# A gated-attention and low-rank-mixer kernel: another opening of the first batch, later loads of two weights, and an unspread closing of the last batch

## The chip, the cores and the metric

The kernel runs on one core of one Trainium2 chip. The time is device microseconds of one execution; the runs below are repeated executions of one program. Five engines work side by side, each with its own queue of instructions in program order: PE (matrix products, which write to PSUM), ACT and DVE (elementwise work, which read PSUM and SBUF), POOL (here it only issues transfers and fills small tiles) and SP (here it issues transfers, above all transposing ones). An instruction that waits for a semaphore holds up everything behind it on its own engine.

## The reference

Eight batches of 3136 rows; `u` and `v` are 256 wide, `z` 64 wide. All are float32 in memory.

```python
# per batch: attention without a softmax, gated by u
scores = (1 / S) * matmul(z, z.T)              # 3136 x 3136, symmetric
attn   = maximum(scores, 0.0) ** 2
x      = u * matmul(attn, v)                   # 3136 x 256
# then a low-rank mixer over the rows, and a two-layer channel network
h   = (x.T @ U @ V).T                          # rank 32
y   = x + h
out = y + maximum(y @ w_ch1, 0.0) @ w_ch2      # 256 -> 1024 -> 256
```

## The kernel before, in words

**Tiles.** The 3136 rows are 25 tiles: 24 full ones of 128 rows and a tail of 64. Row `p * 24 + t` of the first 3072 is row `p` of tile `t`. Everything is computed in bfloat16 with float32 sums.

**Panels and strips.** `attn` is symmetric, so the kernel makes only half of it. The panel of tile `j`, `A[j]`, holds the blocks of row tile `j` against column tiles `j` to `j + 12`, around the circle of 25. A step of `score` (L288 to L313) makes one piece of a panel: two matmuls into a pair of PSUM banks (L298), each using one half of PE's 128 rows, since `z` is 64 wide and stands twice in `zT`; then ACT's relu with the scale (L311) from PSUM to SBUF; then DVE's square in place (L313). There are two such PSUM pairs in turn (`pair_psum`), so the third `score` waits until ACT has read the first. The other half of an output's blocks comes from a strip: `turn` (L333) lets a transposing transfer on SP's queue turn the panel's twelve blocks beside the diagonal into a strip tile.

**Outputs.** Output tile `o` is the sum over 25 tiles `j` of a block (from a panel or from the strip of `o`) times `v[j]`, in matmuls of 64 rows by 256 columns (L371), one half of the rows into each of two PSUM banks. Two neighbouring outputs share a set of two banks; `close_pair` adds the banks (ACT's copy L385, DVE's add L386), multiplies by `u` (L395) and leaves `x_bf`. There are two such sets, `sets[0]` and `sets[1]`. Outputs go in the order 12, 13, ..., 24, 0, ..., 11 (`turns`). Output 24 is the tail and runs as quarters (L405).

**Opening of batch 0** (`start_up`, L665). Seven matmuls on zeros; two thirds of `z` arrive as float32 by two transfers on SP's queue (`first_z`, L212), are cast and doubled by DVE (L215) and ACT (L216), and turned by PE against a unit matrix (`turn_on_pe`, L223); the last third comes through POOL's queue (`load_z`, L174). Outputs 12 to 15 are then summed over all 25 `j` from blocks that are made for them alone: for each pair in `pairs` one `score` of 512 columns for each `j`, against the columns of tiles 12 to 15. Blocks that belong to a panel go to their place in it; the others go to `rooms`, borrowed space in panels that are made later, and are made again when their panel is. The weights (`fetches`, L254 to L261) and the first parts of batch 1's `v` are loaded in this stretch, through POOL's queue. A one-row transfer on SP's queue (`mark`) waits for the third of these parts, and the strips stand behind it. Outputs 16 to 19 follow from stored panels and strips; batch 1's `z` is doubled (L188) and turned (L195) meanwhile.

**The rest.** From output 20 on, `attend_steps` runs output by output, with steps that make later panels spread among the sums (`first_at`, `own_at`, `next_at`), and with the mixer of the batch before in bursts: `up_steps` (L563, relu L571, L579 and L581) and `down_steps` (L610, the add L624, the store L637). A strip is turned four outputs ahead.

**Closing.** The last batch's own mixer has no attention beside it. `rank` (L462) makes `x.T @ U`, `mix` (L515, L522) corrects the turned `x` of chunk 0, and `low_rank` (L531, L545) adds the low-rank part to the `x` of a chunk in PSUM and SBUF and turns it for the up steps. Which PSUM banks `low_rank` uses, and where it stands among the up and down steps, is written out by hand:

```python
for c in range(NC + 1):
    up, down = last[c]
    steps = _merge(up, down)
    adds = {0: ((2, 2),), 1: ((0, 1), (3, 6))}.get(c, ((c + 2, 2),) if c + 2 < NC else ())
    for n, at in reversed(adds):
        steps.insert(at, lambda n=n: low_rank(b, n, other, n > 0))
    run(steps)
```

So chunk 0's add stands after chunk 1's first up step, in the banks of `other`. Two of chunk 0's four up steps (`alone`) use the banks of `spare()` instead of a `pair_psum`. The last chunk's down steps (`apart`) keep their two tiles in separate banks, with an add and a store for each.

Of the kernel before, what the change touches and what calls it, by code (L numbers as in the profile page):

```python
# [7 lines left out]
FP32 = mybir.dt.float32  # L8
# [34 lines left out]
def kernel(  # L43
# [17 lines left out]
    P = 128  # L61
# [138 lines left out]
    def first_z(parts):  # L200

        z_bf = z_tiles[0] = stage.tile([P, NT, 2, dqk], BF16, name="z_bf")
        wide = zT_rest[:, :4, :].rearrange("p t c -> p (t c)")
        nc.vector.memset(wide, 0.0)
        ps = pair_psum()
        for _ in range(7):
            mm(out=ps[:, 0, :], lhsT=zT_rest[:, 0, :], rhs=wide, start=True, stop=True)  # L207
        landed = []
        for t0, t1 in parts:
            z_f = u_pool.tile([P, 2, D], FP32, name="u_sb").rearrange("p a c -> p (a c)")  # L210
            z_f = z_f.rearrange("p (t c) -> p t c", c=dqk)
            nc.sync.dma_start(out=z_f, in_=rows(z[0])[:, t0:t1, :])  # L212
            landed.append(z_f)
        for (t0, t1), z_f in zip(parts, landed):
            nc.vector.tensor_copy(out=z_bf[:, t0:t1, 0, :], in_=z_f)  # L215
            nc.scalar.copy(out=z_bf[:, t0:t1, 1, :], in_=z_f)  # L216

    def turn_on_pe(parts, banks):

        z_bf = z_tiles[0]  # L220
        for (t0, t1), ps in zip(parts, banks):
# [8 lines left out]
            copy = nc.vector.tensor_copy if t0 % 8 or t1 == NF else nc.scalar.copy  # L230
# [21 lines left out]
    def weight_steps():  # L252
        def wide(w_bf, w):
            pool_dma(out=w_bf, in_=w.rearrange("(t p) d -> p t d", p=P))  # L254
# [19 lines left out]
        def copies():  # L274
            for n in (R, 2 * R):
                nc.vector.tensor_copy(out=V_bf[n : 2 * n, :], in_=V_bf[:n, :])

        fetches = [
            lambda: wide(w1_bf, moe_w_ch1),
            narrow,  # L280
            fetch,
            lambda: wide(w2_bf[:, NH // 2 :, :], moe_w_ch2[H // 2 :, :]),
            lambda: wide(w2_bf[:, : NH // 2, :], moe_w_ch2[: H // 2, :]),
        ]
# [302 lines left out]
    def down_steps(b, c):  # L587
# [10 lines left out]
        apart = b == B - 1 and c == NC - 1  # L598

        def step(n, k):  # L600
# [3 lines left out]
            ps = spare()[n] if apart and k else hold[0]  # L604
# [12 lines left out]
            if apart or k == len(pair) - 1:  # L617
                k0 = k if apart else 0
                t, nk = pair[k0], k + 1 - k0
                if k0 == 0:  # L620
                    hold[1] = out_pool.tile([P, 2, D], FP32, name="o_sb")
                o_sb = hold[1][:, k0 : k + 1, :]
                p = P if t < NF else TAIL
                nc.vector.tensor_tensor(  # L624
                    out=o_sb[:p].rearrange("p t (a c) -> p t a c", c=P),
                    in0=split(ps[:p, k0 * D : (k + 1) * D]),
# [9 lines left out]
                if t < NF:  # L636
                    store(out=rows(out[b])[:, t : t + nk, :], in_=o_sb)  # L637
                else:
                    store(out=out[b, NF * P :, :], in_=o_sb[:TAIL, 0, :])
# [24 lines left out]

    def start_up():  # L665
        parts = ((8, 16), (0, 8), (16, NF))
        first_z(parts[:2])
# [10 lines left out]
        load_v(0, (8, 12))  # L678
        load_v(0, (12, 18))
        load_z(0, parts[2:])  # L680
        for part in [(3, 8), (0, 3), (18, NF), (NF, NT)]:
            load_v(0, part)
        turn_on_pe([(8, 12), (12, 16)], sets[0])
        turn_on_pe([(0, 4), (4, 8)], sets[1])
        nc.gpsimd.memset(U_bf[:, NF, :], 0.0)
        outs = [FIRST + i for i in range(NG)]
        c0 = FIRST * P
        for o in outs[::2]:
            open_pair(0, o)
            load_u(0, o)  # L690
        if B > 1:
            load_z(1, WHOLE)
        run(fetches)
        if B > 1:
            for part in V_PARTS[:3]:
                load_v(1, part)
        nxt = [s for j in range(LEAD, LEAD + NG) for s in turned(0, j)]
        rooms = [A[j % NT][:, : 2 * NG * P] for j in range(LEAD + NG, LEAD + 3 * NG)]
        rooms = [r.rearrange("p (a w) -> p a w", a=2) for r in rooms]
        pairs = [(8, 9), (10, 11), (12, 13), (14, 15), (6, 7), (3, 4), (5,), (1, 2)]  # L700
        pairs += [(0, 16), (17, 18), (19, 20), (21, 22), (23, 24)]
        where = {}
        mark = small.tile([P, D], BF16, name="mark", tag="t1_sb")[:1, :8]

        def make(pair):
            if all(LEAD - 1 - HALF <= j < FIRST for j in pair):
                todo = []
                for j in pair:
                    at = (FIRST - j) * P
                    where[j] = A[j][:, at : at + NG * P]  # L710
                    todo.append((j, c0, NG * P, where[j]))
                score(0, todo)
            else:
                room = rooms.pop(0)
                for i, j in enumerate(pair):
                    where[j] = room[:, i, :]
                score(0, [(j, c0, NG * P, room) for j in pair])

        def use(pair, some):
            for j in pair:  # L720
                for o in some:
                    at = (o - FIRST) * P
                    stop = [o % 2 == 1 and j == NF - h for h in range(2)]
                    beside(o, j, where[j][:, at : at + P], stop)

        for i, pair in enumerate(pairs):
            if i == 5 and B > 1:

                nc.sync.dma_start(out=mark, in_=v_both[1][:1, V_PARTS[2][1] - 1, :8])
            if i == 3:  # L730
                double_z(0, parts[2:])
            if i == 5:
                turn_on_pe([(16, NF)], [pair_psum().rearrange("p a w -> p (a w)")])
                turn_on_pe([(NF, NT)], [pair_psum()[:, 0, :]])
                extend_z(0)
            make(pair)
            if i > 5 and i % 2:
                nxt.pop(0)()
            if i > 1:
                use(pairs[i - 2], outs)  # L740

        for o in outs[1::2]:
            nxt.pop(0)()
            for pair in pairs[-2:]:
                use(pair, (o - 1, o))
            close_pair(0, o)

        outs = [LEAD + i for i in range(NG)]
        for o in outs[::2]:
            open_pair(0, o)  # L750
            load_u(0, o)
        pairs = [(j, j - 1) for j in range(LEAD - 1, LEAD - FIRST, -2)]

        def use_stored(js, some):
            for j in js:
                for o in some:
                    if 0 <= o - j <= HALF:
                        beside(o, j, block(0, o, j))

        def make_stored(pair):  # L760
            todo = []
            for j in pair:
                k0, k1 = LEAD - j, min(NB, LEAD + NG - j)
                todo.append((j, LEAD * P, (k1 - k0) * P, A[j][:, k0 * P : k1 * P]))
            score(0, todo)

        nxt += [lambda pair=pair: make_stored(pair) for pair in pairs[:2]]
        run(nxt[:2])
        own = [
            lambda j=j, some=some: use_stored([j], some)  # L770
            for some in (outs[:2], outs[2:])
            for j in outs
            if j <= some[-1]
        ]
        run(_merge(nxt[2:], own))
        rest = []
        for j in reversed(range(FIRST - NG, LEAD)):
            rest += score_steps(0, j, LEAD + NG - j, NB)
        more = [s for j in range(LEAD + NG, LEAD + 2 * NG - 1) for s in score_steps(0, j)]
        for i, pair in enumerate(pairs):  # L780
            if i + 2 < len(pairs):
                make_stored(pairs[i + 2])
            else:
                more.pop(0)()
            use_stored(pair, outs)
            if B > 1 and i in (1, 2):
                part = ((0, FIRST), (FIRST, NF))[i - 1]
                double_z(1, (part,))
                turn_z(1, (part,))
            if i == len(pairs) - 1:  # L790
                turn(0, LEAD + NG)
        tail = []
        for o in outs:
            js = [(o + 1 + i) % NT for i in range(HALF)]

            def close(o=o, j=js[-1]):
                beside(o, j, block(0, o, j), [o % 2 == 1] * 2)
                if o % 2:
                    close_pair(0, o)
                if o == outs[1]:  # L800
                    load_u(0, LEAD + NG)
                if o < outs[-2]:
                    turn(0, o + NG + 1)

            for i in range(3):
                some = js[4 * i : min(4 * i + 4, HALF - 1)]
                tail.append(lambda o=o, js=some: [beside(o, j, block(0, o, j)) for j in js])
            tail.append(close)
        for s in _merge(tail, more + rest):
            s()  # L810
# [134 lines left out]
```

## Time and profile before

| | |
|---|---|
| Runs (us) | 1000.08, 1001.38, 1001.78; median 1001.38 |
| The profiled execution's own time | 1000.08 |
| Its span on the core | 998.3 |
| PE, ACT, DVE, POOL busy | 983.4, 612.2, 551.1, 171.7 |
| PE busy from 0 to 5 / 5 to 10 us | 3.75 / 4.04 |
| PE busy from 30 to 35 / 35 to 40 us | 5.00 / 4.94 |
| PE busy from 60 to 80 / 80 to 100 us | 19.45 / 20.00 |
| First cast of `z` (L215, L216) | 3.54 |
| First score pair (L298) | 6.06 |
| Closing of outputs 12-13 / 14-15 on ACT (L385) | 24.16 / 25.40 |
| First strip issued on SP's queue (L333) | 29.84 |
| Last closing of outputs 16-19 on ACT | 44.38 |
| Closing of output 24 on ACT | 65.39 |
| First matmul of `w2` (L610) | 123.88 |
| Last batch's first `rank` matmul (L462) | 943.48 |
| Issue of the last store | 995.38 |

Times count from the start of the span. PE's busy time is modelled and covers the pipeline's latency, so a window in which PE is full can still hold small gaps; a window in which it is not full holds a wait. A row of the profile gives the engine, the line, the operation, the tiles as `out<-in`, the shape, and in brackets how long the engine stood idle before it and what ended that. The numbers of a window are its length, then busy time and instructions of PE, PEld (the loading of PE's weights), DVE, ACT and POOL, the granted clock, the mean busy share of the transfer engines and GB/s.

### The profile page before, as it was taken

Reading aid. Unit: us, or ns where it says so; the run is one execution under the profiler, and the core shown is the slowest. Engines: PE = TensorE matmul, PEld = TensorE weight load, DVE = VectorE, ACT = ScalarE, POOL = GpSimd, SP = SyncE. Lnnn points to the kernel's source line nnn. Section 1 sums busy time; section 2 is a strip of 40 time slices with the busy share of each in tenths; the row PEclk is TensorE's granted clock in tenths of the full one; section 3 lists DMA queues with packets and bytes.
Section 4 is the critical chain, followed back from the end, with each engine's and each line's share of the span. In section 5 each row is a group of like instructions: output and inputs, shape, how many; then the busy total and the mean of one; then the engine's idle time right before and its main releaser. Section 6 shows DMA issues by size and latency. Waiting matters only on the chain.

```text
span 998.3 us, 31020 instructions
## 1 busy us (share of the span) xinstructions
PE 983.4 (99%) x13688; PEld 776.5 (78%) x13688; DVE 551.1 (55%) x1003; ACT 612.2 (61%) x835; POOL 171.7 (17%) x317
## 2 busy tenths in 40 slices
PE   8899999999999999999999999999999999999998
PEld 6678777787778877788787887878877788787866
DVE  6878754467444665456644566445664457542352
ACT  8877764667645776466754667556674666643154
POOL 5111112111121211221112211112111120011000
PEclk9999999999999999999999999999999999999999
DMA  9999989899798999999999997989979998678533
GB/s 195 185 195 204 174 156 186 185 176 173 153 198 171 169 157 186 179 178 169 160 180 176 181 168 149 188 174 177 175 151 194 166 188 159 120 150 161 129 95 101
DMA packets 414790, 167.94 MB, mean 168 GB/s; under 512 B 389488, under 2 KB 399408, under 8 KB 414656
## 3 DMA queue, kind: packets, MB, share of 16 engines
q1 hardware_dynamic: 385424, 99.68, 62.3%
q0 software_dynamic: 29232, 66.28, 28.3%
q8 instruction: 107, 1.75, 0.7%
q14 instruction: 27, 0.22, 0.1%
HBM read 61.88 MB, written 25.69 MB: 88 GB/s over the span
## 4 chain that ended last, share of the span: by engine, by line
PE 91%; DVE 4%; ACT 3%; DMA 1%; issue 1%; POOL 0%; DVEq 0%; POOLq 0%
PE ps L371 47%; PE ps L563 17%; PE ps L610 17%; PE ps L298 6%; ACT A L311 2%; DVE A L313 2%; PE ps L405 1%; PE ps L531 1%; DVE x_bf L545 1%; DMA out_dram<-o_sb 1%; DMA strip<-A 1%; DVE both L386 1%; PE ps L479 1%; DVE x_bf L395 1%; PE ps L207 0%
## 5 line engine op out<-in xcount | busy, mean ns | idle before, releaser
L311 ACT ACTIVATE A<-ps 128x832 bf16<-128x832 f32 (+9 forms) x477 | 358.9, 769 | 155.4 <-PE ps L298 148.1
L371 PE MATMUL ps<-v,A 64*128 64x256 bf16 x4988 | 341.6, 269 | 1.8 <-DVE A L313 1.1
L313 DVE TENSOR_TENSOR A<-A 128x832 bf16<-128x832 bf16 (+9 forms) x477 | 244.7, 527 | 133.1 <-ACT A L311 130.0
L371 PE MATMUL ps<-v,strip 64*128 64x256 bf16 x4420 | 307.3, 269 | 3.4 <-DMA strip<-A 2.5
L371 PEld LDWEIGHTS <-A 64*128 64x128 bf16 x4988 | 246.3, 94 | 45.4 <-issue 10.0
L581 ACT ACTIVATE relu_bf<-ps 128x1024 bf16<-128x1024 f32 (+2 forms) x206 | 186.2, 911 | 140.0 <-PE ps L563 139.8
L371 PEld LDWEIGHTS <-strip 64*128 64x128 bf16 x4420 | 222.6, 94 | 37.2 <-DMA strip<-A 3.9
L624 DVE TENSOR_TENSOR o_sb<-ps,x_bf 128x512 f32<-128x512 f32 (+2 forms) x105 | 69.9, 665 | 243.7 <-PE ps L610 221.7
L610 PE MATMUL ps<-w_bf,relu_bf 128*128 128x256 bf16 (+1 forms) x1600 | 201.2, 273 | 0.0
L563 PE MATMUL ps<-ut,w_bf 128*128 128x512 bf16 (+2 forms) x896 | 198.6, 353 | 0.0
L610 PEld LDWEIGHTS <-relu_bf 128*128 128x128 bf16 (+1 forms) x1600 | 153.0, 98 | 45.6 <-issue 3.6
L563 PEld LDWEIGHTS <-w_bf 128*128 128x128 bf16 x896 | 84.9, 98 | 62.0 <-issue 6.9
L355 POOL DMA_DIRECT2D u_sb<-in_u_dram x96 | 53.7, 559 | 456.1 <-DVE x_bf L395 441.9
L298 PE MATMUL ps<-zT 64*128 64x416 bf16 (+8 forms) x812 | 131.6, 312 | 0.0
L385 ACT COPY both<-ps 128x512 f32<-128x512 f32 (+1 forms) x104 | 58.9, 566 | 72.9 <-PE ps L371 66.6
L637 POOL DMA_DIRECT2D out_dram<-o_sb x84 | 46.0, 548 | 276.2 <-DVE o_sb L624 272.9
L386 DVE TENSOR_TENSOR both<-ps,both 128x512 f32<-128x512 f32 (+1 forms) x104 | 69.3, 667 | 28.2 <-ACT both L385 27.5
L395 DVE TENSOR_TENSOR x_bf<-both,u_sb 128x512 bf16<-128x512 f32 (+1 forms) x104 | 69.8, 672 | 3.7
L545 DVE TENSOR_TENSOR x_bf<-ps,x_bf 128x512 bf16<-128x512 f32 (+1 forms) x112 | 65.5, 626 | 7.2 <-PE ps L531 7.1
L298 PEld LDWEIGHTS <-zT 64*128 64x128 bf16 x812 | 43.1, 94 | 4.0
L244 POOL DMA_DIRECT2D v<-in_v_dram x61 | 34.1, 561 | 0.8 <-DMA w_bf<-in_moe_w_ch_dram 0.7
L298 PE MATMUL ps<-relu_bf 64*128 64x416 bf16 (+9 forms) x121 | 22.2, 333 | 3.9 <-ACT A L311 3.3
(54 smaller groups left out, 208.0 us busy)
## 6 DMA issues: line engine op xcount, KB each, us to landing
u_sb<-in_u_dram POOLq DMA_DIRECT2D x96, 256.0 KB, 4.1
out_dram<-o_sb POOLq DMA_DIRECT2D x84, 256.0 KB, 3.3
v<-in_v_dram POOLq DMA_DIRECT2D x57, 192.0 KB, 4.8
strip<-A SPq DMA_TRANSPOSE x196, 5.5
out_dram<-o_sb SPq DMA_DIRECT2D x11, 256.0 KB, 2.0
z_c<-in_z_dram POOLq DMA_DIRECT2D x7, 384.0 KB, 5.9
u_sb<-in_u_dram POOLq DMA_DIRECT2D x16, 64.0 KB, 2.5
ut<-x_bf SPq DMA_TRANSPOSE x56, 3.7
```

What stands on the lines that cost most here:

```text
L298: mm(out=ps[:, k, :n], lhsT=zT[halves[k], j, :], rhs=zT_flat[halves[k], c : c + n], start=True, stop=True,)
L311: nc.scalar.activation(out=dst, in_=src, func=AF.Relu, scale=sc)
L313: nc.vector.tensor_tensor(out=dst, in0=dst, in1=dst, op=ALU.mult)
L371: mm(out=acc[t0][h][:, (o - t0) * D : (o - t0 + 1) * D], lhsT=w[halves[h]], rhs=v_both[b % 2][halves[h], j, :], start=start, stop=stop, **kw,)
L385: nc.scalar.copy(out=both[:, :w], in_=banks[1][:, :w])
L386: nc.vector.tensor_tensor(out=both[:, :w], in0=banks[0][:, :w], in1=both[:, :w], op=ALU.add)
L395: nc.vector.tensor_tensor(out=x_at(b, t0, n), in0=split(both[:, :w]), in1=u_sb[:, :n, :].rearrange("p t (a c) -> p t a c", c=P), op=ALU.mult,)
L545: nc.vector.tensor_tensor(out=q, in0=split(ps[h][:, : len(ks) * D]), in1=q, op=ALU.add)
L563: mm(out=ps[i][:, :w] if apart else ps[:, i, :w], lhsT=w1_bf[:, db, (hp + i) * P : (hp + i + 1) * P], rhs=uT[c][:, db, len(chunks[c]) * P ...
L581: nc.scalar.activation(out=relus[c][:, hp : hp + 2, :w], in_=ps[:, :, :w], func=AF.Relu)
L610: mm(out=ps[r, k * D : (k + 1) * D], lhsT=relus[c][:, ht, q : q + (TAIL if two else P)], rhs=w2_bf[:, ht, :], start=(ht < 1 + two), stop=( ...
L624: nc.vector.tensor_tensor(out=o_sb[:p].rearrange("p t (a c) -> p t a c", c=P), in0=split(ps[:p, k0 * D : (k + 1) * D]), in1=x_at(b, t, nk) ...
```

## The change

The opening is written anew. `first_z` sends all of `z` by SP's and ACT's queues in turn, the tail too, and its casts come back as steps. Outputs 12 to 15 no longer get blocks of their own: their panels 12 to 15 are made in full, then the needed ends of panels 11 to 0, and tiles beyond each panel come from the strips of outputs 12 to 15, turned on SP's queue as soon as each panel is squared. `rooms` and `mark` are gone. Outputs 16 to 19 follow in the same way. Batch 1's `z` is doubled and turned at outputs 21 to 23 (steps 9 to 11 of the main loop) instead of in the opening. `w1` is fetched at output 7 (step 20), into the space of batch 0's `zT`, and two DVE copies at output 10 (step 23) put its columns in another order; `w2` is fetched in batch 1, eight neighbouring rows to each partition, in the order that fits those columns. In the closing, chunk 0's `low_rank` stands behind the first of its own up steps, in the banks of `spare()`, `mix` comes before the late down steps, and the last two tiles share one bank, one add and one store.

In batch 0 the program order has, of score matmuls, 22 fewer of 512 columns and 2 fewer of 448, and 15 more of 64-row shapes between 128 and 416 columns; 92 of the L371 matmuls read a strip instead of a panel; four more strips are turned.

```diff
     def first_z(parts):
...
-            nc.sync.dma_start(out=z_f, in_=rows(z[0])[:, t0:t1, :])
...
+        queues = (nc.sync.dma_start, nc.scalar.dma_start)
+        for n, (t0, t1) in enumerate(parts):
+            if t0 == NF:
+                z_f = both_pool.tile([P, 512], FP32, name="both")[:, :dqk]
+                for r in halves:
+                    queues[n % 2](out=z_f[r], in_=z[0, NF * P :, :])
+                z_f = z_f.rearrange("p (t c) -> p t c", t=1)
+            else:
+                pool, name = ((u_pool, "u_sb"), (out_pool, "o_sb"))[n % 2]
...
+                queues[n % 2](out=z_f, in_=rows(z[0])[:, t0:t1, :])
+
+            def cast(t0=t0, t1=t1, z_f=z_f, shared=n < 2):
+                nc.vector.tensor_copy(out=z_bf[:, t0:t1, 0, :], in_=z_f)
+                copy = nc.scalar.copy if shared else nc.vector.tensor_copy
+                copy(out=z_bf[:, t0:t1, 1, :], in_=z_f)
...
+        w1_tmp = idle[:, : ND * H].rearrange("p (a h) -> p a h", a=ND)
+        def first_w():
+            pool_dma(out=w1_tmp, in_=moe_w_ch1.rearrange("(t p) d -> p t d", p=P))
+        def second_w():
+            pool_dma(out=w2_bf, in_=moe_w_ch2.rearrange("(p t) d -> p t d", t=NH))
+        def order_w():
+            for a in range(ND):
+                nc.vector.tensor_copy(
+                    out=w1_bf[:, a, :].rearrange("p (t q) -> p t q", q=P),
+                    in_=w1_tmp[:, a, :].rearrange("p (q t) -> p q t", t=NH),
+                )
...
-        apart = b == B - 1 and c == NC - 1
...
-            ps = spare()[n] if apart and k else hold[0]
+            ps = hold[0]
...
+    def use_strip(o, part):
+        js = [(o + 1 + i) % NT for i in range(HALF)]
+        for j in js[4 * part : 4 * part + 4]:
+            end = j == js[-1]
+            beside(o, j, block(0, o, j), [end and o % 2 == 1] * 2)
+        if part == 2 and o % 2:
+            close_pair(0, o)
...
     def start_up():
-        parts = ((8, 16), (0, 8), (16, NF))
-        first_z(parts[:2])
+        casts = first_z(((8, 16), (16, NF), (0, 8), (NF, NT)))
...
+        run(casts[:2])
+        turn_on_pe([(8, 12), (12, 16)], sets[0], (act, vec))
+        turn_on_pe([(16, 20), (20, NF)], sets[1], (act, vec))
+        casts[3]()
...
+        run(fetches[:2])
+        panel = {o: turned(0, o) for o in range(FIRST, LEAD + NG + 1)}
...
+        make((8, 9), FIRST)
+        turn_on_pe([(NF, NT)], [sets[1][0]], (vec,))
+        casts[2]()
+        make((10, 11), FIRST)
+        steps = [panel[12][0], use((8, 9)), turn_rest, panel[12][1], use((10, 11))]
+        steps += [lambda: extend_z(0), lambda: make((6, 7), FIRST), panel[13][0], use((12,))]
+        steps += [panel[13][1], use((6, 7)), panel[14][0], use((13,)), panel[14][1]]
+        steps += [panel[15][0], use((14,)), panel[15][1], lambda: make((4, 5), FIRST), use((15,))]
+        steps += [lambda: make((2, 3), FIRST), use((4, 5)), lambda: make((0, 1), FIRST)]
+        steps += [use((2, 3)), *strip_steps(12), panel[16][0], use((0, 1)), *strip_steps(13)[:2]]
+        steps += [panel[16][1], strip_steps(13)[2], *strip_steps(14), panel[17][0]]
...
+    later = {(0, 20): fetches[2], (0, 23): fetches[3], (1, 1): fetches[4]}
...
     rank(b, other[0], 0, NT - 3)
-    run(late[: ups // 2])
+    run(late[: NH // 2])
     rank(b, other[0], NT - 3)
-    run(late[ups // 2 : ups])
+    run(late[NH // 2 : NH // 2 + 1])
     mix(b, 0)
+    run(late[NH // 2 + 1 :])
     low_rank(b, 1, other)
-    run(late[ups:])
     for c in range(NC + 1):
         up, down = last[c]
...
+        if c + 2 < NC:
+            up.insert(3 if c == 0 else 1, lambda c=c: low_rank(b, c + 2, other))
+        if c == 0:
+            up.insert(1, lambda: low_rank(b, 0, None, False))
+        run(_merge(up, down))
```

## The prediction

> **What bounds the kernel now.** I read the page's shares first: PE 99% busy, DVE 55%, ACT 61%, so nearly everywhere only PE's queue counts. Then, since the change lies at both ends, the waits of PE in the first 70 us (line waited for: total us, times, longest) and after them:
>
> ```profile
> PE ps L298 <- ACT A L311: 3.3, 5, 1.0
> PE ps L371 <- DMA strip<-A: 2.5, 1, 2.5
> PE ps L371 <- DVE A L313: 2.0, 4, 0.9
> ...
> PE ps L531 <- DVE x_bf L545: 1.1, 7, 0.2
> ```
>
> Most of what PE loses to waits, it loses in the opening: 3.3 on ACT, 2.0 on DVE, 2.5 on one strip. The windows show where (first PE busy, then PEld, DVE, ACT):
>
> ```profile
> 10.00:15.00 5.00, 4.59 (x72) 3.72 (x70) 4.90 (x11) 3.43 (x8) 3.31 (x6) 1.00 1.11 250
> 15.00:20.00 5.00, 4.40 (x66) 3.43 (x63) 3.26 (x5) 5.00 (x6) 3.36 (x7) 1.00 1.12 207
> 20.00:25.00 5.00, 4.42 (x69) 3.55 (x67) 3.48 (x6) 4.51 (x7) 1.52 (x3) 1.00 1.30 199
> 25.00:30.00 5.00, 3.64 (x38) 1.91 (x36) 4.93 (x10) 5.00 (x9) 1.09 (x2) 1.00 0.77 158
> ...
> 40.00:50.00 10.00, 6.91 (x114) 5.58 (x111) 6.88 (x15) 7.38 (x13) 1.61 (x3) 1.00 1.19 200
> ```
>
> ACT is full at 15-20 and 25-30, where PE has gaps; at 40-50 PE misses 3.1 us while ACT has room. The chain of waits names that gap, the strip of output 20:
>
> ```profile
> 41.20 0.51 DVE A L313
> 41.72 0.03 issue
> 41.75 0.27 DVE both L386
> 42.02 6.45 DMA strip<-A
> 48.47 0.05 issue
> 48.52 0.50 PE ps L371 x6
> ```
>
> Last the closing, in the timeline: PE never stops from 949.5, and the end is one add and one store.
>
> ```profile
> 947.52 1.23 DVE L522 TENSOR_TENSOR ut<-ps,ut 128x1024 bf16<-128x1024 f32 x1
> 948.66 1.28 DVE L545 TENSOR_TENSOR x_bf<-ps,x_bf 128x512 bf16<-128x512 f32 x2
> ...
> 994.93 0.42 DVE L624 TENSOR_TENSOR o_sb<-ps,x_bf 128x256 f32<-128x256 f32 x1 [0.52 <-PE ps L610]
> ```
>
> **The change, part by part.** Durations used: a long run of L371 matmuls takes 0.87 us per 16, so 0.0545 each; ACT on a 1024-wide PSUM pair 0.90 from start to start (three in 2.70), on 512 columns 0.48 (6.54, 7.04, 7.51, 7.99), 832 between them by width, 0.75, with 0.86 to its end; PE's score to ACT's start 0.4 (6.06 to 6.54; 48.86 to 49.24); the square of 832 0.59, of 512 0.42.
>
> *Work.* In batch 0 the order of instructions has 22 fewer score matmuls of 512 columns and 2 fewer of 448, and 15 narrower ones in their place: 6,912 columns less, two row halves at once, 3,456 / 2.4 per ns = 1.4 us of PE. ACT drops nine 1024s, four 512s and an 896 (10.8) and gains nine narrower (4.9): 5.9 us less. The 92 matmuls that go from panels to strips cost the same. None of this is a gain yet: what counts is when each queue gets through.
>
> *z.* The second piece goes out on ACT's queue at 0.80 instead of 1.24 on SP's. ACT issues three transfers before its table load. By SP's rows (0.39, 0.42) that is 1.2 us:
>
> ```profile
> 0.80 1.28 ACT L216 ACT_TABLE_LOAD   x1 [0.80 <-PEq L929]
> 0.80 0.86 SPq L212 DMA_DIRECT2D u_sb<-in_z_dram  x2
> 3.54 1.25 ACT L216 CAST z_bf<-u_sb 128x512 bf16<-128x512 f32 x2 [1.46 <-DMA u_sb<-in_z_dram]
> ```
>
> The cover is the 1.46 us that ACT idles for z: 1.2 fits with 0.2 left, price 0. Both z pieces now share the engines, so the first lands up to 0.6 later (the distance of the two landings before, 3.5 and 4.1), and the cast with it. Bounds: -0.4 (the saved issue) to +1.3 (cover gone, PE and all else waits for ACT's half of the cast); I take +0.3, near the late side of the landing.
> [...]
>
> *First four outputs (12-15).* I walked the queues from the first score pair at 6.06. The second pair now follows two 64-column casts on DVE (0.24 and 0.21, row L272), behind the copy that ends at 6.86: 7.3 instead of 6.3. The turn of z tiles 0-7 holds one of two PSUM pairs until DVE's 1024-column copy (1.22) ends at 11.4; ACT idles 1.1 and begins panel 13's stretch at 11.9. In panels 13-15 each later half stands on PE behind matmuls that read the half just made: 0.4 + 0.86 + 0.59 and 6, 4 or 2 matmuls, 2.2 a panel against 1.5 of ACT alone. So panel 15 is squared at 19.4, the last narrow pair leaves ACT at 21.6, and strips begin at 21.9: 4 x 23 strip matmuls and 6 others (5.3) and four score pairs (0.7) end at 28.0. Before, these outputs' accumulators close at 25.4. That is 2.6 later, but with panels 12-17 stored, most of which were made afterwards before.
>
> *Outputs 16-19.* 196 matmuls (10.7), 20 score pairs (3.1), and 3.2 of waits: the second accumulator set is free only after ACT's copy and DVE's add (28.3 + 0.58 + 0.69), and the two closings (1.3 each on DVE) hold back squares that PE is next in line for. End 45.0 against 43.95.
>
> *Outputs 20-24.* Strip 20's panel is squared at 38.5 instead of 42.0, so the 2.5 wait goes, and the one at 57.5 (1.2, strip 23). Before, 43.95 to 65.4 is 21.4; after, 21.4 - 2.5 - 1.2 - 0.4 (narrower panels 0-2, no panel 23) = 17.3. End 62.3 against 65.4: **-3.1**. What is late next: batch 1's z is doubled and turned at outputs 21-23 instead of in the opening, so DVE's copy of zT (L238) may wait some 3 us for its transfer. Behind it stand the squares of panels 6-11, the add of output 24, and ACT's copies L391; PE meets that only at the third score after it. Price 0, up to 2.
>
> *Strips under load.* Four strips now start at 12-20 us, beside POOL's loads of v, u, z, U and V. Issue to landing (min/median/max), for the strips issued at 29-41, no loads beside them, and at 76-92, loads beside them:
>
> ```profile
> DMA to landing us min/median/max: 3.8/5.3/5.9
> DMA to landing us min/median/max: 5.6/7.7/9.8
> ```
>
> Strip 12 goes out at 12.0 and is wanted at 21.9; 13 at 15.1 for 23.7; 14 at 17.4 for 25.2; 15 at 19.5 for 26.6. At 7.7 each all land in time (14 just); at 9.8 strips 14 and 15 are 2 to 3 late. w1 and w2, 1 MB between 19.4 and 26.1, are gone from here, which helps. I take +0.6, between 0 and 7.
>
> *w1, w2 late.* w1 lands in 7.0 (its rows before: 6.9 to 7.3) and is reordered three outputs later (3.1 each, 9.3). The reorder is two strided DVE copies, 1.1 each by the 768-column L265 row (0.82), beside gaps of about 1 us per square at 95-100; if that cover is gone, 2.2. w2 is wanted at the first L610 (123.9) and issued near 105. POOL's queue behind both holds u and v loads with a pair's lead. 0.
>
> *Closing.* Output chunk 0's adds move in front of its second up step, which uses the same two banks. DVE then has in order: the mix add (ends 949.5), an output add (0.69), chunk 1's two adds and chunk 0's two (0.60 apart): the bank is free at 951.9, PE wants it at 950.6. The wait of 1.3, less 0.1 of slack, is +1.2. PE, then all ups and downs, stand behind it. The last two tiles leave as one 512-wide add and one 256 KB store: 0.69 for 0.42, and 1.9 to 2.1 to landing for 1.7: +0.5. Together **+1.7**, bounds 0.5 (DVE ahead of my count) to 2.6.
>
> **Sum.** 0.3 - 3.1 + 0.6 + 1.7 = -0.5 on the profiled execution, 998.3 of span and 1.8 around it, 1000.08: 999.6. That execution was the fastest of three; their median is 1001.38, 1.3 higher. For a median of runs I name 1000.7.
>
> **Rivals.** *Faster:* ACT is the true bound of the opening. Then most of its 5.9 counts, say 5.0, and with z +0.3 and the closing's 1.7 the time is 3.0 lower: 1000.7 - 2.5 = 998.2, from there down to 996.8 if the closing costs only its 0.5. For it: ACT full at 15-20 and 25-30. Against it: my walk finds ACT idling about 4 us before 21.6, on DVE and PSUM.
> *Slower:* strips 13-15 come late. Strips issued at 77.9, 81.9 and 83.8 under load landed about 4 us apart; were 13, 14 and 15 to follow strip 12 (19.7) in such steps, 15 would land at 31.7, 5.1 after it is wanted. It decides once the steps exceed (26.6 - 19.7) / 3 = 2.3. Time 1000.7 + 5.1 - 0.6 = 1005.2. For it: DMA share 1.1 to 1.3 at 10-25. Against it: the landings with no loads beside them are 1.3 to 2.1 apart, and POOL's backlog should be gone by about 21.
> *It does not do what it says* (opening unchanged in time, later outputs waiting for strips as before): then only the closing shows, 1002.7. The earlier issue of strip 20 speaks against it.
>
> **How the numbers follow.** Forecast (the opening's gain and the closing's loss cancel to within a microsecond or two) 0.38; faster 0.28; slower by late strips 0.24; closing alone 0.10. About 0.2%, 2 us, is what a measurement here can tell from no change. "Closing alone" lies 1.3 above the median, so I count 0.06 of it within and 0.04 beyond: faster 0.28, same 0.38 + 0.06 = 0.44, slower 0.24 + 0.04 = 0.28. The range reaches to both rivals, 996.8 to 1005.2; the forecast's own is 998.7 to 1002.7.
>
> **What would show it.** Right: the accumulators of 12-15 close near 28, no wait of PE on a strip, first matmul of output 20 near 45, output 24's end near 62; near 950 a wait of PE's up step on L565's adds of about 1.2. Wrong: PE waiting for a strip between 22 and 28 (the slower rival), accumulators closing at 26 or sooner (the faster one), the first cast after 4.0 (the table load), DVE stalled at the reorder near 97.

## The result: 2.4% slower

The changed kernel takes 1026.07 us (median of 6 runs, 1021.51 to 1028.71) against 1000.88 (999.5 to 1004.02): ratio 1.0241, 95% interval 1.021 to 1.0272. The forecast was 1000.7. The profiled run of the changed kernel is its fastest, 1021.51 (span 1019.5).

First the waits of PE, as they were shown for before (line <- what it waited for: total us, times, longest):

```profile
PE ps L391 <- DMA strip<-A: 5.8, 4, 3.7
PE ps L425 <- DVE x_bf L565: 5.6, 5, 4.4
PE ps L318 <- ACT A L331: 2.8, 5, 1.1
PE ps L391 <- DVE A L333: 2.8, 6, 0.8
...
PE ps L583 <- DVE x_bf L565: 1.0, 1, 1.0
```

Strips are waited for four times instead of once (at 42.4, 56.9, 108.5 and 113.9 us; none of them at 22 to 28), and a new wait of 4.4 stands before L425, the matmuls of output 24, here of batch 1. The windows show where PE goes empty (PE, PEld, DVE and ACT busy; then POOL, granted clock, DMA share, GB/s):

```profile
15.00:20.00 5.00, 3.31 (x32) 1.67 (x32) 4.04 (x8) 5.00 (x9) 0.45 (x1) 0.88 1.29 144
20.00:25.00 5.00, 5.00 (x75) 4.64 (x73) 0.96 (x4) 1.49 (x4) 0.00 (x0) 0.77 1.21 253
...
40.00:50.00 10.00, 8.84 (x145) 7.33 (x144) 7.58 (x15) 7.80 (x13) 1.63 (x3) 1.00 1.18 220
100.00:110.00 10.00, 7.16 (x120) 5.89 (x115) 5.92 (x9) 4.88 (x7) 1.62 (x3) 1.00 1.31 132
110.00:120.00 10.00, 6.26 (x89) 4.27 (x88) 2.03 (x4) 2.41 (x4) 0.00 (x0) 0.83 1.09 160
160.00:200.00 40.00, 35.35 (x407) 26.74 (x405) 14.50 (x28) 15.99 (x23) 7.10 (x13) 0.91 0.87 152
```

At 40-50 PE gained 1.9 on before's 6.91, as forecast. But at 100-120 it misses 6.6 and at 160-200 4.7, where before had full rows. At 100-110 the DMA engines were busy (1.31) and moved only 132 GB/s. The chain of waits puts one strip there, and DVE's timeline three waits on late transfers. After the last of them come the low-rank adds (L565, from 179.10), and then PE's wait of 4.4:

```profile
96.35 17.54 DMA strip<-A
113.89 0.05 issue
```

```profile
66.22 0.56 DVE L250 COPY zT<-zT 128x1536 bf16<-128x1536 bf16 x1 [3.00 <-DMA zT<-z_bf]
...
102.50 2.10 DVE L277 COPY w_bf<-relu_bf 128x1024 bf16<-128x1024 bf16 x2 [2.56 <-DMA relu_bf<-in_moe_w_ch_dram]
...
178.63 0.56 DVE L250 COPY zT<-zT 128x1536 bf16<-128x1536 bf16 x1 [5.56 <-DMA zT<-z_bf]
```

```profile
179.84 0.37 PE L425 MATMUL ps<-v,A 64*64 64x256 bf16 x1 [4.42 <-DVE x_bf L565]
```

Waiting is not all of the loss. PE's busy time is 989.7 us against 983.4, although it has a little less to do. The granted clock of the changed kernel stood at 0.50 for 3.4 us from 18.8, for 3.4 from 114.4 and for 6.8 from 179.3, and at 1.00 otherwise from 6 us to the end of its last matmuls; before had 1.00 from 6 to 990. At 0.50 a 64x256 matmul of L391 took a mean of 412 ns (20.0 to 22.2), at 1.00 it took 269 from a strip (22.3 to 24.5). Half of these 13.6 us, 6.8, is an estimate of what the slower clock added to the 21.2 by which the span grew.

To place the loss, take for each pair of outputs the time at which DVE writes it to `x_bf` (L415; L395 before), changed minus before. Pair 0 is outputs 12 and 13 of batch 0, pair 6 is output 24, pair 13 begins batch 1, pair 103 is the last.

| pair | 0 | 1 | 3 | 5 | 6 | 11 | 13 | 17 | 18 | 20 | 103 | span |
|---|---|---|---|---|---|---|---|---|---|---|---|---|
| changed - before | +2.1 | +2.9 | +1.7 | -0.8 | +2.7 | +1.6 | +10.5 | +10.5 | +14.7 | +18.2 | +19.0 | +21.2 |

Four steps: +3.5 at output 24 (batch 1's z; 1.3 of it is gone again at pair 7), +8.9 at pairs 12 and 13 (w1, issued at 89.2), +7.7 at pairs 18 to 20 (batch 2's z, which the change also moves: loaded at output 17 of batch 1 instead of 13, and doubled and turned later), and +2.2 in the closing. At w1 PE waited 1.8 (the profile names no releaser), 1.0 and 3.7, and then had the clock of 0.50 for 3.4 us; at batch 2's z it waited 4.4 and had that clock for 6.8: with half of the slow time each, the same estimate, 8.2 and 7.8. The opening itself stands at -0.8.

### The profile page after: what moved, and what is told of

Read it like the earlier page. It is cut to its first block, busy times and chain, and to the rows that moved or that the text cites. A ratio compares the mean times of both kernels' runs of the same rounds, so it can differ in the third digit from the quotient of the medians.

```text
span 1019.5 us, 30998 instructions
## 1 busy us (share of the span) xinstructions
PE 989.7 (97%) x13679; PEld 781.2 (77%) x13679; DVE 549.0 (54%) x1002; ACT 605.1 (59%) x829; POOL 168.9 (17%) x313
## 4 chain that ended last, share of the span: by engine, by line
PE 86%; DMA 7%; DVE 5%; ACT 2%; issue 0%; ACTq 0%; DVEq 0%; SPq 0%
PE ps L391 43%; PE ps L628 17%; PE ps L583 17%; PE ps L318 6%; DMA strip<-A 4%; DMA zT<-z_bf 3%; ACT A L331 2%; DVE x_bf L565 1%; DVE A L333 1%; PE ps L425 1%; PE ps L551 1%; DVE both L406 1%; PE ps L499 1%; DVE x_bf L415 1%; DMA both<-in_z_dram 1%
## 5 line engine op out<-in xcount | busy, mean ns | idle before, releaser
L331 ACT ACTIVATE A<-ps 128x832 bf16<-128x832 f32 (+9 forms) x472 | 352.3, 761 | 166.1 <-PE ps L318 153.3
L391 PE MATMUL ps<-v,A 64*128 64x256 bf16 x4896 | 339.7, 271 | 3.0 <-DVE A L333 2.8
L391 PE MATMUL ps<-v,strip 64*128 64x256 bf16 x4512 | 314.0, 269 | 7.6 <-DMA strip<-A 5.8
L333 DVE TENSOR_TENSOR A<-A 128x832 bf16<-128x832 bf16 (+9 forms) x472 | 240.7, 523 | 136.6 <-ACT A L331 133.4
L391 PEld LDWEIGHTS <-A 64*128 64x128 bf16 x4896 | 243.8, 95 | 47.3 <-issue 10.0
L391 PEld LDWEIGHTS <-strip 64*128 64x128 bf16 x4512 | 229.6, 94 | 41.1 <-DMA strip<-A 6.9
L639 DVE TENSOR_TENSOR o_sb<-ps,x_bf 128x512 f32<-128x512 f32 (+1 forms) x104 | 69.7, 670 | 242.3 <-PE ps L628 220.6
L583 PE MATMUL ps<-ut,w_bf 128*128 128x512 bf16 (+2 forms) x896 | 198.3, 353 | 1.1 <-DVE x_bf L565 1.0
L583 PEld LDWEIGHTS <-w_bf 128*128 128x128 bf16 x896 | 85.2, 98 | 63.2 <-issue 7.8
L406 DVE TENSOR_TENSOR both<-ps,both 128x512 f32<-128x512 f32 (+1 forms) x104 | 69.3, 667 | 28.8 <-ACT both L405 28.2
L415 DVE TENSOR_TENSOR x_bf<-both,u_sb 128x512 bf16<-128x512 f32 (+1 forms) x104 | 69.8, 672 | 3.6
L565 DVE TENSOR_TENSOR x_bf<-ps,x_bf 128x512 bf16<-128x512 f32 (+1 forms) x112 | 65.4, 626 | 8.2 <-PE ps L551 8.0
L551 PE MATMUL ps<-t_sb,V_bf 64*128 64x256 bf16 x200 | 22.8, 270 | 1.1 <-DVE x_bf L565 1.1
```

The costliest lines, as they stand in the source:

```text
L331: nc.scalar.activation(out=dst, in_=src, func=AF.Relu, scale=sc)
L333: nc.vector.tensor_tensor(out=dst, in0=dst, in1=dst, op=ALU.mult)
L391: mm(out=acc[t0][h][:, (o - t0) * D : (o - t0 + 1) * D], lhsT=w[halves[h]], rhs=v_both[b % 2][halves[h], j, :], start=start, stop=stop, **kw,)
L406: nc.vector.tensor_tensor(out=both[:, :w], in0=banks[0][:, :w], in1=both[:, :w], op=ALU.add)
L415: nc.vector.tensor_tensor(out=x_at(b, t0, n), in0=split(both[:, :w]), in1=u_sb[:, :n, :].rearrange("p t (a c) -> p t a c", c=P), op=ALU.mult,)
L565: nc.vector.tensor_tensor(out=q, in0=split(ps[h][:, : len(ks) * D]), in1=q, op=ALU.add)
```

## Experiments

My first theory took these steps as separate. Four kernels tried them one by one.

**Weights in the opening** (e1): `fetches` as in before, no reorder.

```
...
-        run(fetches[:2])
+        run(fetches)
...
-    later = {(0, 20): fetches[2], (0, 23): fetches[3], (1, 1): fetches[4]}
```

> The changed kernel (1026.1 median) with w1 and w2 fetched in the opening in before's layouts, without the reorder; all else as changed. Theory (w1's megabyte among the strips of 89 to 114 us and the reorder behind it cost the 8.7 that output pairs 12 to 13 and later close late): pairs 13 to 17 close about 9 earlier than in the changed kernel (+1.5 to +2 against before in place of +10.5), time 1017, ratio to before 1.016; strips issued at 89 to 97 land in at most 10 us. Rival A (the megabyte costs the same wherever strips are in flight; in the opening it falls on strips 12 to 15): outputs 12 to 15 close 5 to 9 later than the 28.0 of the changed kernel and time stays at 1022 to 1026. Rival B (what is lost at 95 to 114 is lost to something else, the loads of u and v or the lower clock): pair 13 still at +10, time 1026.

1025.3, ratio 1.0234 (1.0201 to 1.0267). Pairs 11 to 17 all stand at +11.3: the step at pair 13 is gone, but pair 0 is at +9.7. Rival A holds. Later in this profile output stores came late (pair 103 at +28.2); why stays open.

**z early** (e2): batch 1's z doubled and turned between outputs 16 and 19, batch 2's conditions as in before.

```
...
-                if b and i == (1 if b > 1 else 5):
+                if b and i == 1:
...
-                    if n == (1 if b > 1 else 3):
+                    if n == 1:
```

> The changed kernel with z of batch 1 doubled and turned in the opening's second half, and z of batch 2 loaded, doubled and turned at before's places; the weights late, as changed. Theory (DVE waits with its queue for the late turned z: 3.5 at output 24, 7.7 in batch 1): pair 6 closes near -0.5 to 0 against before in place of +2.7, and pairs 18 to 20 gain nothing on pair 17, so time 1026.1 - 10 = 1016, ratio 1.015; no DVE wait of 3.0 at 66 and of 5.6 at 178. Rival (these waits only take the place of others behind them, strips or scores): at least half comes back, time 1021 or more. The weights' step at pair 13 should stay at +7 to +9 in either.

1026.01, ratio 1.0236 (1.0197 to 1.0275). The steps at output 24 and at pairs 18 to 20 are gone (pairs 5 and 6 both +10.9; pairs 15 to 20 all +19.3), as is that at pair 13. But pair 0 stands at +9.3, although up to there the order of instructions is that of the changed kernel, and a step of 8.4 appears at pair 15, where w2 and batch 2's z are now in flight together (issued 117.2 to 118.7, landed by 131.3). Neither theory nor rival had this. Both also expected the step at pair 13 to stay: here w1, still fetched late (issued at 98.3), landed after 9.2 instead of 13.3, and no step is left at pair 13.

**The closing alone** (e3), the changed closing put into before:

> Before with the changed closing alone (low-rank adds of the last batch in front, last chunk's tiles in pairs). Theory: PE's wait for the bank 1.1 and the longer last add and store, together 2.2 as in the changed kernel: 1003.1, ratio 1.002. Prediction's term: +1.7, 1002.6. Rival (the loss at the end there was the lower clock of 0.97 at 1000 to 1020, not the order): below +0.7, ratio under 1.001.

1005.06, ratio 1.0034 (1.002 to 1.0049). A loss, but 1.8 of this profile's lag arises in the opening, which the edit does not touch; d1 below measures it better.

**The opening alone** (e4): the edits of e1 and e2 and before's closing together.

> The changed kernel's opening (strips from their own panels, z by two queues), with weights, z of batches 1 and 2 and closing as before. Theory (the opening by itself is about neutral): between -3 and +1 against before, 998 to 1002. Rival (strips with the weights beside them are late in the opening): outputs 12 to 15 close 5 or more after 28.0, and time is 1005 or more, ratio over 1.004.

1016.25, ratio 1.0144 (1.0112 to 1.0176): the rival. Pair 0 is at +11.2, pair 3 at +16.1, pairs 5 to 28 at +12.7. So the -0.8 above is not what this opening usually gives; whether the execution, the chip or something else made the difference is not shown, for the changed kernel has one profile. The first strip shows it:

| profile | strip 12 issued, landed | strip 15 landed | pair 0 |
|---|---|---|---|
| changed | 12.55, 20.9 | 26.8 | +2.1 |
| e2, same instructions so far | 12.24, 27.3 | 31.7 | +9.3 |
| e1, weights beside | 14.24, 28.6 | 33.1 | +9.7 |
| e4, weights beside | 14.07, 29.1 | 33.5 | +11.2 |

PE in e2 then waits in one piece:

```profile
27.35 2.74 PE L391 MATMUL ps<-v,strip 64*128 64x256 bf16 x23 [6.46 <-DMA strip<-A]
```

The DMA view of 14 to 24 us shows what was under way. GB/s comes in 40 slices of 0.25 us; q0 are POOL's loads, q1 SP's strips, each with packets, MB and the time of its packets as a share of 16 engines; the issue rows end with the median from issue to landing. Before (no strips in flight), then e2:

```profile
GB/s 385 340 328 279 213 262 184 213 219 185 223 172 193 190 228 209 201 201 209 221 193 191 221 211 227 233 290 161 183 104 177 203 198 178 205 182 195 199 197 195
...
U_bf<-in_moe_U_dram POOLq DMA_DIRECT2D x1, 192.0 KB, 7.2
```

```profile
GB/s 299 180 213 213 197 221 197 173 213 229 98 60 81 134 306 48 29 49 40 126 13 29 11 26 123 62 31 4 35 9 74 71 63 169 85 35 15 13 126 98
DMA packets 2016, 1.05 MB, mean 105 GB/s; under 512 B 1782, under 2 KB 1869, under 8 KB 2015
...
q1 hardware_dynamic: 1570, 0.40, 69.7%
q0 software_dynamic: 445, 0.63, 57.6%
...
U_bf<-in_moe_U_dram POOLq DMA_DIRECT2D x1, 192.0 KB, 12.7
strip<-A SPq DMA_TRANSPOSE x3, 13.0
```

In before the loads alone moved a mean of 215 GB/s and landed in 6.7 to 7.2. In e2, with transposes beside them, the packets of both took 69.7 + 57.6% of the engines' time, the mean was 105 GB/s, 15 of the 40 slices stood at 4 to 49, and both kinds landed in 12.4 to 13.0. In the changed kernel's own profile the same stretch falls to 0 to 10 GB/s for about 1 us and then recovers. This is the new theory: transposes and loads in flight together.

A transposing strip also held SP's queue while it was being issued, strips 12 to 15 of the changed kernel for 2.10, 3.72, 3.30 and 1.28 us, and a strip behind another started late. Panel 15 was squared at 18.9 in the changed kernel and 18.5 in e2, but strip 15 was issued at 22.95 (strip 14, issued at 19.5, had held the queue until 22.8) and 28.03. Beside w1 the same shows (88 to 104 us; ns min/median/max to issue one, in the changed kernel, then in c2 below, where strips are copies):

```profile
L353 SPq DMA_TRANSPOSE strip<-A x4: 1451/3927/8725, 85.8 to 96.3; - x4
```

```profile
L113 SPq DMA_DIRECT2D strip<-A x5: 464/465/465, 90.2 to 102.3; - x5
```

To test the theory without transposes, each transpose was replaced by a copy of the same bytes on the same queue, in before (c1) and in the changed kernel (c2); in c3 and c4 the copies have 256-byte packets, like the transposes (0.40 MB in 1570 packets in e2's view above; 1.22 MB in 4862 in c4's). The copies leave out the transposing, so the output is not the reference's; and they change two things at once, the landing and the hold on SP's queue.

```
-    transpose = nc.sync.dma_start_transpose
+    def transpose(out, in_):
+        ...
+        nc.sync.dma_start(out=out, in_=in_.rearrange("p (t c) -> p t c", c=P))
```

> Before, with every transpose on SP's queue (strips, z, the mixer's x) replaced by a plain copy of the same bytes between the same tiles, one 3 KB row to a partition for a strip: the output is not the reference's, since the strips are not transposed; every other instruction and wait is kept. It is the base for the changed kernel in the same form. Theory (PE is the bound of before, its strips are in time): 996 to 1001. Rival (before too is held back by its transposes): under 995.

> The changed kernel with the same replacement (output not the reference's). Theory (the loss is transposes in flight beside POOL's loads; a copy in rows has no such clash): against before in this form, pair 0 closes at +1 to +2.5, no step over 2 at pairs 11 to 14 (w1) and at most 3 at pairs 18 to 20 (z of batch 2), and the two differ by the closing's 2.8 and 0 to 3 more: 3 to 6 in place of 25. Rival A (it is bytes: any transfer on SP's queue beside the loads): pair 0 at +6 or more or a step of 6 or more at pair 13, difference 12 or more. Rival B (the order of waits on DVE and PE, not the transfers): the step of about 7 at pairs 18 to 20 stays, difference 9 to 12.

> Before with plain copies again, but each split in two transfers of every second tile, so that the packets are 256 bytes, the size that the transposes' packets have (output not the reference's). Theory (transposing, not packet size): within 3 of the copies in rows. Rival (many small packets): 1000 or more, as before.

> The changed kernel with copies in 256-byte packets (output not the reference's). Theory (transposing): 3 to 6 above before in this form, pair 0 at +1 to +2.5. Rival (256-byte packets beside 1 to 4 KB packets of the loads are the clash, whether they transpose or not): strip 12 takes over 8, pair 0 at +6 or more, difference 12 or more.

| form | before | changed | difference | pair 0 | pair 5 | pair 6 | pair 13 | pair 20 | pair 103 |
|---|---|---|---|---|---|---|---|---|---|
| transposes | 1000.88 | 1026.07 | 25.2 | +2.1 | -0.8 | +2.7 | +10.5 | +18.2 | +19.0 |
| 256-byte copies | 997.33 | 1008.42 | 11.1 | +1.2 | +0.1 | +4.1 | +2.8 | +7.4 | +7.4 |
| row copies | 995.86 | 1000.61 | 4.8 | -0.1 | -0.1 | +1.3 | 0.0 | +1.4 | +1.4 |

The first columns are medians, the pairs are from the profiles. Ratios to the kernel before: c1 0.9952 (0.9934 to 0.9971), c2 0.9976 (0.9946 to 1.0005), c3 0.996 (0.9941 to 0.998), c4 1.0081 (1.0059 to 1.0104). With rows, the theory's numbers come, but for pair 0, which is at -0.1 instead of +1 to +2.5. Strip 12 lands at 19.3, strip 15 is issued at 18.87, and the same 14 to 24 us read:

```profile
DMA packets 1189, 2.48 MB, mean 248 GB/s; under 512 B 368, under 2 KB 496, under 8 KB 1188
...
strip<-A SPq DMA_DIRECT2D x3, 384.0 KB, 5.5
...
U_bf<-in_moe_U_dram POOLq DMA_DIRECT2D x1, 192.0 KB, 6.4
```

w1's step of 8.9 is gone in both forms, though w1 itself still takes 11.1 with rows (84.45 to 95.6): in these profiles that step comes only with transposes, and e2 shows that it does not always come with them. In 256-byte packets the steps of z stay (+4.0 at pair 6, +4.6 by pair 20), so c4's "3 to 6" failed, and its rival's 12 is not quite reached, though both halves of strip 12 took 9.6, over the rival's 8: what z loses is not a matter of transposing alone. Beside its second step the granted clock stood at 0.50 for 3.4 us from 168.9 in c4 and at 1.00 in c2 (means of the whole profiles 0.997 and 1.0); half of that time, 1.7, is an estimate of its part. Before, too, is some 5 faster without transposes (0.9952), between what theory and rival expected of c1.

Four last runs took the rest apart, in these quieter forms. **The closing** on c1 (d1), **all of z on SP's queue** in c2 (d2), **z early and before's closing** in c2 (d3), **z early** in c4 (d4):

```
-        queues = (nc.sync.dma_start, nc.scalar.dma_start)
+        queues = (nc.sync.dma_start, nc.sync.dma_start)
```

> Before with the changed closing alone, transposes as copies in rows (output not the reference's; runs in this form repeat to 0.6). Theory: PE's wait for the bank 1.1 and the longer last add and store cost 2.0 to 2.6 together on the 995.9 of before in this form: 998.1. Prediction's term 1.7: 997.6. Rival (the 2.8 of the closing alone with transposes was spread of the runs): under 997.

998.14 (ratio 0.9933, 0.9913 to 0.9953; all its pairs are within 0.1 of c1's): the closing costs 2.3, theory. These four runs come from another chip than c1 to c4. The kernel before had medians of 1003.16 (1000.24 to 1007.47) and 1002.51 (998.5 to 1012.74) beside them, too wide for such differences: by the ratios d1 would be faster than c1. The profiles are clearer: d1's span is 2.4 longer than c1's, all of it behind pair 103.

> The changed kernel with copies in rows and all of z on SP's queue, in the same order of pieces. Theory (two z pieces in flight together land together and late: first cast 4.38 in place of 3.56): first cast at 3.5 to 3.7, pair 0 closes 0.5 to 0.9 earlier, and 0.5 of it reaches the end, 1000.1 in place of 1000.6. Rival A (the opening hangs on ACT or on the strips, not on z): pair 0 moves less than 0.3, time 1000.6. Rival B (the third and fourth pieces on SP come later and hold the turn of tiles 0 to 7 and the tail): pair 0 later, time over 1001.

1004.38 (1.0006, 0.9988 to 1.0024), 3.8 above c2: rival B. The first cast came at 3.54, as wanted, but the 16 KB tail, issued at 2.82 instead of 1.78, landed at 11.9 instead of 6.8, with five loads of v sent out by POOL from 1.43 to 4.26, and the third piece, issued 0.5 later, landed 4.6 later. PE shows it as one wait, at the turn of the tail, and runs on at a granted clock of 0.50 until 15.8; that turn took 0.29 (0.23 in c2, where the clock was at 1.00):

```profile
12.31 0.29 PE L241 MATMUL ps<-eye,z_bf 128*128 128x128 bf16 x1 [5.86 <-DVE z_bf L231]
```

> The changed kernel with copies in rows, z of batches 1 and 2 at before's places and before's closing; the strip opening, z by two queues and the late weights stay. Theory (what is left of the change is free when its transfers don't clash): pairs 5 to 14 at -0.2 to 0 against before in this form, pairs 18 to 20 at 0, time 995.9 to 996.5. Rival (w2 and z of batch 2 beside each other at 110 to 135, the step of 8.4 at pair 15 of the earlier run): a step of 1 or more at pair 15, time 997 to 999.

998.42 (0.9941, 0.9918 to 0.9965). The steps at pairs 15 and 18 to 20 are absent, but the opening stands at +1.2 from pair 4 to the end. By its time this is the rival's 997 to 999, by its steps not: opening and early z together are not quite free. Against c2 the lag is 0.6 at pairs 0 and 1, where both still have the same order; there the granted clock stood at 0.50 from 7.8 to 11.2 us in d3 and at 1.00 in c2 (means of the whole profiles 0.998 and 1.0). The other 0.6 comes at pairs 2 and 3, beside the early z.

> The changed kernel with copies in 256-byte packets and z of batches 1 and 2 at before's places; weights late and closing as changed. Theory (the late turned z holds DVE's queue, 2.7 at pair 6 and 4.6 at pairs 18 to 20): both steps go, 1008.4 - 7.3 = 1001.1. Rival (the wait passes to the strips of outputs 20 to 24 or to w2 beside z of batch 2): half or more comes back, 1004.5 to 1009.

1000.62 (0.9967, 0.995 to 0.9985), 7.8 below c4: theory. DVE's waits on zT (the copy in `extend_z`), in c4 and then in d4:

```profile
DVE zT L263 <- DMA zT<-z_bf: 8.1, 4, 3.5
```

```profile
DVE zT L263 <- DMA zT<-z_bf: 0.9, 2, 0.6
```

Not measured: a guard like `mark` in the changed kernel; later loads of U, V and batch 1's z, and w1 without its reorder, both beside true transposes; and before without `mark`. No experiment points to a version faster than before.

## Why the prediction failed

- **"w1, w2 late", 0: the step that failed in the profiled execution, with batch 2's z below.** The step looked at DVE's gaps for the reorder. The reorder did wait 2.6 and take 2.1, but strips issued at 89.4 to 96.4 took 13.2 to 17.5, PE waited for them, and pair 13 was 8.9 later against before than pair 11. With row copies the same reorder at the same place cost nothing (pair 13 at 0.0).
- **"Strips under load", +0.6, between 0 and 7: held in that execution, failed in three others.** In the changed kernel's profile strips 12 to 15 landed at 20.9, 23.5, 24.9 and 26.8, wanted at 21.9, 23.7, 25.2 and 26.6, and PE did not wait for them. Their landing was taken from strips at 76 to 92 (5.6 to 9.8), beside small loads of u and v. In the opening, beside 0.86 MB of POOL's loads from 14 to 24 us (0.63 in e2), the changed kernel, e2, e1 and e4 gave 8.4, 15.1, 14.4 and 15.0 for strip 12. That a strip's issue holds SP's queue, here for 1.28 to 3.72 us, was not in the sum. The slower rival had the place right, but priced it at 5.1 from steps of 4 us between the strips, while these three close pair 0 by 9 to 11 late. That e2 lands strip 15 at the 31.7 it named is luck: strips 12 to 15 came there at 27.3, 28.6, 30.0 and 31.7. The removed `mark`, which held before's strips until the loads had landed, was never priced; that it is the cure is argued, not shown.
- **Batch 1's z, "price 0, up to 2":** the 3.0 wait of DVE came as described, and PE met it after all with waits of 0.7 and 1.1. The 3.5 at output 24 is largely DVE's own delay; 2.2 remain at pair 7. **Batch 2's z** was in the change and missing from the sum: 7.7. e2 and d4 remove both steps; only d4 has the time back.
- **Outputs 12 to 19** closed as walked in the changed kernel's profile (+2.1 to +2.9, forecast +2.6; then +1.1 to +1.7, forecast +1.05). From there to output 23 the lag fell by 2.5, where the walk had 4.1: strip 20's wait of 2.5 went, but PE waited 0.8 for DVE at 48.3, and the wait at 57, read as 1.2, was 0.9 in before and 0.6 after. So ACT's closing of output 24 came 0.8 earlier (64.61 for 65.39) instead of 3.1. The faster rival fell: with row copies pair 5 was at -0.1, in the changed kernel at -0.8.
- **Closing, +1.7:** right mechanism (L583's wait of 1.0 in the changed kernel), 2.3 in size.
- **Work, 1.4 us of PE**, stands in no term of the sum. Its 2.4 columns per ns is what L298's rows give in before: a mean of 376 ns for 512 columns and 189 for 64, so 448 columns in 187. That two row halves run at once is in the 0.0545 us from one 256-column matmul to the next, half of the 0.107 that 2.4 per ns gives for one.
- **The granted clock** is in no term of the sum. It was at 0.50 for 13.6 us of the changed kernel's profile, some 6.8 of the loss by the estimate above.
- **The sum itself** has two slips: 999.6 and 1.3 make 1000.9, not 1000.7, and the closing alone on a median of 1001.38 makes 1003.1, not 1002.7. Neither bears on the miss.
- **z by two queues, +0.3:** the first cast was 0.8 late. The three issues moved ACT's table load by 1.66 (0.80 to 2.46), not 1.2:

```profile
2.46 1.28 ACT L226 ACT_TABLE_LOAD   x1 [2.46 <-issue]
4.31 0.62 ACT L226 CAST z_bf<-u_sb 128x512 bf16<-128x512 f32 x1 [0.57 <-DMA u_sb<-in_z_dram]
```

The table load ended at 3.74, and ACT then waited 0.57 for z, which landed at 4.31: the cast came after 4.0, but the landing held it, not the table load. Little issue time is saved by the second queue, 0.5 to 1.0 by d2. What it was worth there is the landing, 4.6 earlier for the third piece and 5.1 for the tail; that these had a place ahead of POOL's backlog is the author's reading.

## What to carry to other kernels

Before moving a transfer, look at what is in flight on every queue when it runs, and take its landing time from a stretch with the same company, not from the nearest row of the same kind. A transfer that seems to do nothing but wait may be what keeps two kinds of traffic apart, so price its removal. When one profile shows a good opening, take another before trusting it: the same order of instructions closed its first pair at +2.1 and at +9.3. And read the granted clock beside the waits: here an estimated 6.8 us of the 21.2 lie in stretches at 0.50.

## What the runs showed of the hardware

- From 18 to 22 us POOL's loads alone moved 202 GB/s (before); with transposes beside them loads and strips together moved 144 and 46 (changed, e2); with 256-byte copies 172 (c4), with row copies 317 (c2). A transpose packet took a mean of 71 ns in e2 from 14 to 24 us (1570 packets, 69.7% of 16 engines) and 22 in the changed kernel (4337, 58.3%); from 30 to 37 in before, with 0.18 MB of loads beside them, it took 30 (3674, 99.1%).
- Issuing a transposing strip held SP's queue for 3.72 us in the changed kernel's opening (strip 13), for 1.28 there at 22.95 (strip 15) and for 8.7 beside w1 (96.35). In c2 a copy in rows held it some 0.47 in the same stretches.
- PE's granted clock stood at 0.50 from 18.8 to 22.2, from 114.4 to 117.8 and from 179.3 to 186.1 in the changed kernel. The stretch at 114.4 began 0.5 after PE's wait of 3.7 had ended, the one at 179.3 within its wait of 4.4 (175.42 to 179.84). At 20-25 the mean was 0.77 though PE was busy throughout (5.00 of 5.00). What set these stretches off is not shown.
- Runs with row copies repeat within 0.7, 1.6 and 2.5 us (c1, c2, d2); those of the changed kernel spread over 7.2, those of before over 4.5 beside them and 14.2 beside c1 to c4.
